# Sparse attention and a routed MLP on one core: batch 0 with a pair's values one pair behind its scores, v of batches 2 and 3 loaded behind the weights, values woven denser with w1 matmuls

## The chip, the cores and the metric

The kernel runs on one core of a Trainium2 chip. The metric is the device time of one execution in microseconds (us). A core has five engines that run their own instruction streams in order: TensorE (PE, matmuls and transposes), VectorE (DVE), ScalarE (ACT), GpSimd (POOL) and SyncE (SP). Here POOL issues all loads from HBM, through one DMA queue, and SP issues the stores and a few copies inside SBUF, through another.

## The reference

There are 4 batches, 8 heads of 64, and 768 positions. Each position attends to its neighbours closer than 16 and to 24 summaries, one per block of 32 positions (the maximum of the block's keys, the mean of its values, each weighted by 32). The 8 heads side by side make x of 768 x 512. The mean of x over the positions picks one of 8 experts per batch, and the output is a two-layer MLP of that expert.

```python
k_sum = k.reshape(B, H, nb, block, D).max(axis=3)
v_sum = v.reshape(B, H, nb, block, D).mean(axis=3)
...
scores_all = np.concatenate([scores_l_m, scores_s], axis=-1)   # window of 16 each way, and 24 summaries
...
a = a / (np.sum(a, axis=-1, keepdims=True) + 1e-09)
x = np.matmul(a, np.concatenate([v, v_sum], axis=2))           # then heads side by side
...
e_idx = np.argmax(x.mean(axis=1) @ w_gate, axis=1)             # one expert a batch
out[b] = gate_w[b] * (np.maximum(x[b] @ w1[e], 0.0) @ w2[e])
```

## The kernel before

The schedule is written out by hand: every step is a Python closure that emits instructions for several engines, and the order in which the closures are called is the order on each engine. `run` calls a list of steps; `weave(main, fill)` calls the steps of `main` and spreads those of `fill` evenly behind them.

Heads are worked on in pairs (4 pairs a batch), positions in two halves of 384 (`u`). The steps of a batch `b` are:

- `T_k(b, pr)`, `T_q(b, pr)`: 16 PE transposes into PSUM (`kps`, `qps`), and a copy out (`kaug`, `qT`; ACT, or for part of the keys of later batches DVE).
- `K_rest`: on DVE the block maxima of the keys (`kmx`, L271) and three copies that complete `kaug` (halos and summaries, L277 to L283).
- `S_tile(b, pr, u)`: scores in PSUM (`sc`: the mask by L350, the products by L362), then the exponential on ACT into `aT` (L372).
- `V_sum`: block sums of the values on PE (`vsps`, L300) and a DVE cast (L309). `V_copy(b, pr)`: a DVE copy of those sums into the rows of `vblk` that the values matmul reads (L315).
- `O_tile(b, pr, u)`: 12 matmuls of `aT` with `vblk` (`ops`, L386), then on DVE the reciprocal (`rv`, L394) and the product (`xs`, L397).
- `X_tile`: three PE transposes of `xs` (`xps`, L413), and an ACT copy into `xT` that also sums over positions (L414).
- `gate(b)`: 8 small matmuls (`lgps`, L427), the expert's index on DVE, and then POOL issues the loads of that expert: `w1` in four pieces (L453), whatever `between` says, and `w2` in two (L457).
- `H_chunk` (16 a batch: 4 matmuls, `hps`, L492, and a relu on ACT, or on DVE for one in four, L501) and `O_chunk` (12 a batch: 4 matmuls, `o_ps`, L515; every second one scales and stores 128 rows).

`vblk` holds values as rows of 64 positions with a halo of 16 rows on either side. For batch 0 the values come pair by pair (L104), and the halo rows are copied inside SBUF by SP (`halo`, L125 and L129) once a pair's values have landed. For later batches POOL loads the values in two halves (L104) and then both halos from HBM (L114, L118): `load_vs`. There are two `vblk` and two `kaug` buffers; `edges` writes their constant rows. PSUM has 2 buffers for `sc` and 4 for all else.

`warm` issues matmuls on a tile of zeros; their results are overwritten. Batch 0 is attention alone; from batch 1 on, the attention of batch `b+1` is woven with the MLP of batch `b`, and the MLP of batch 3 ends the program. After the last `gate` nothing is woven.

Of the kernel before, what the change touches and what calls it, by code (L numbers as in the profile page):

```python
# [22 lines left out]
def kernel(  # L23
# [10 lines left out]
    nc = tc.nc  # L34
# [105 lines left out]
    load_q(0, 0, 2)  # L140
    load_v(0, 0, 2)
# [14 lines left out]
    load_k(0, 2, 4)  # L156
    load_q(0, 2, 4)
    load_v(0, 4, 6)
    load_v(0, 6, 8)
    for pr in range(2, NP):  # L160
        load_k(0, 2 * pr, 2 * pr + 2)
        load_q(0, 2 * pr, 2 * pr + 2)
# [6 lines left out]
    def edges(i):  # L169

        nc.vector.memset(vblks[i][0:QB, :, :, D:DP], 1.0)
        nc.vector.memset(vblks[i][R_SUM:NR, :, :, D:DP], float(BLK))
        nc.vector.memset(vblks[i][QB:R_SUM, :, :, D:DP], 1.0)
        nc.vector.memset(vblks[i][QB:R_SUM, :, 0:1, 0:D], 0.0)
        nc.vector.memset(vblks[i][QB:R_SUM, :, NJ - 1 : NJ, 0:D], 0.0)
        nc.vector.memset(kaugs[i][:, :, 0:1, R_PRE:R_POST], 0.0)
        nc.vector.memset(kaugs[i][:, :, NJ - 1 : NJ, R_POST:R_SUM], 0.0)
        nc.vector.memset(kaugs[i][:, :, :, NR:128], 0.0)

    edges(0)  # L180
# [109 lines left out]
    def V_sum(b, prs):  # L290
        def f():
            vb = vblks[b % NV]
            if b == 0:
                halo(b, 2 * prs[0], 2 * prs[-1] + 2)
            vs_ps = one_pool.tile([128, 2, D], FP32, name="vsps", tag="one")
            if b == 0:
                warm(vs_ps.rearrange("p h c -> p (h c)"), 2, 128)
            for j in range(NJ):
                for pr in prs:
                    nc.tensor.matmul(  # L300
                        vs_ps[BLK * pr : BLK * (pr + 1), :, :],
                        lhsT=bind[:, j, :],
                        rhs=vb[0:QB, 2 * pr : 2 * pr + 2, j, 0:D],
                        start=(j == 0),
                        stop=(j == NJ - 1),
                    )
# [28 lines left out]
    def S_tile(b, pr, u):  # L335
        def f():
# [3 lines left out]
            if b == 0:  # L340
# [34 lines left out]
    def O_tile(b, pr, u):  # L375
        def f():
# [3 lines left out]
            if b == 0:  # L380
                warm(ops.rearrange("p t h c -> p (t h c)"), 1)
# [165 lines left out]
    a0 = [first_warm, T_k(0, 0), *pair_keys(0)]  # L547
    for pr in range(NP):
        more = pr + 1 < NP
        a0 += [S_tile(0, pr, 0), S_tile(0, pr, 1)]  # L550
        a0 += [T_k(0, pr + 1)] if more else []
        a0 += [O_tile(0, pr, 0), O_tile(0, pr, 1)]
        a0 += pair_keys(pr + 1) if more else []
        a0 += [X_tile(0, pr, 0), X_tile(0, pr, 1)]
# [48 lines left out]
    run(s1[:14])  # L603
# [50 lines left out]
```

## Time and profile before

| | |
|---|---|
| median of 2 runs | 195.38 us (194.44 to 196.32) |
| the profiled execution: its time, and its span | 196.97 us, 194.9 us |
| PE busy, share of the span | 165.7 us, 85% |
| DVE, ACT, POOL busy | 92.6 us, 91.8 us, 47.1 us |
| mean granted clock of PE | 0.939 |
| last gate matmul starts, batch 0, 1, 2, 3 | 39.21, 78.15, 119.86, 159.21 us |

Times in the views are microseconds from the start of the span. A row of the timeline gives the start, the length, the engine, the line, the operation, its tiles (out<-in), how many instructions are merged (x12), and in brackets the idle time of that engine before it and what ended the wait. The four gates cut the execution into stages: batch 0 alone, three stages in which attention of one batch is woven with the MLP of the one before, and the rest of the MLPs.

### The profile page before, as it was taken

The page shows a single profiled execution, that of the slowest core. Times are in us where ns is not written, and L with a number is a line of the kernel's source. Part 1 is how long each engine was busy: PE and PEld are TensorE (multiplying, and loading weights), DVE is VectorE, ACT ScalarE, POOL GpSimd, SP SyncE. Part 2 cuts the span into 40 slices and gives each one's busy share as a digit, 9 for nine tenths or more (in the row PEclk, how much of TensorE's full clock was granted, in tenths as well). Part 3 has the DMA queues.
Part 4 walks back from the last instruction along what each step waited for, and adds up shares of the span by engine and source line. Part 5 has one row for each costly group of instructions (what it writes and reads, how often), then busy time and mean ns, then how long its engine had stood idle before and what let it go on. Part 6 is the DMA issues. An engine that isn't in the chain of part 4 may idle for free.

```text
span 194.9 us, 5234 instructions
## 1 busy us (share of the span) xinstructions
PE 165.7 (85%) x2242; PEld 95.9 (49%) x2257; DVE 92.6 (47%) x249; ACT 91.8 (47%) x187; POOL 47.1 (24%) x65
## 2 busy tenths in 40 slices
PE   7497988859987698989959998799969989979991
PEld 2355556547444365455525565455635644545440
DVE  5625475475036463768214853975257533121211
ACT  2132656748764066265831555466634651436120
POOL 7980000049700000497000000990000008000000
PEclk9998599975699799999996999999999999999999
DMA  4999950019999996399999991799998016999142
GB/s 45 149 172 222 215 93 3 0 20 139 158 101 95 203 207 120 57 151 187 194 123 200 206 175 62 111 157 203 177 157 148 3 55 105 168 274 156 54 161 108
DMA packets 57382, 26.00 MB, mean 133 GB/s; under 512 B 39696, under 2 KB 54288, under 8 KB 57360
## 3 DMA queue, kind: packets, MB, share of 16 engines
q0 software_dynamic: 52992, 19.00, 112.4%
q1 hardware_dynamic: 4368, 6.68, 11.4%
q8 instruction: 17, 0.28, 0.6%
q14 instruction: 5, 0.04, 0.1%
HBM read 38.00 MB, written 6.29 MB: 227 GB/s over the span
## 4 chain that ended last, share of the span: by engine, by line
DMA 36%; PE 35%; POOL 8%; issue 8%; DVE 5%; ACT 4%; POOLq 2%; SPq 0%; DVEq 0%; ACTq 0%
DMA vblk<-in_v_dram 27%; PE hps L492 12%; PE o_ps L515 8%; DMA w_sb<-in_moe_w_dram 6%; PE ops L386 5%; DMA vblk<-vblk 3%; POOL w_sb L453 3%; POOL vblk L104 3%; PE xps L413 2%; ACT xT L414 2%; PE vsps L300 2%; PE sc L229 1%; ACT qT L250 1%; ACT o_sb L530 1%; POOLq L439 1%
## 5 line engine op out<-in xcount | busy, mean ns | idle before, releaser
L492 PE MATMUL hps<-xT,w_sb 128*128 128x384 bf16 x256 | 50.7, 344 | 1.5 <-DMA w_sb<-in_moe_w_dram 1.3
L515 PE MATMUL o_ps<-w_sb,hT 128*128 128x512 bf16 x177 | 43.9, 380 | 1.6 <-issue 1.3
L453 POOL DMA_DIRECT2D w_sb<-in_moe_w_dram x16 | 12.0, 760 | 115.4 <-DVE grec L468 55.3
L503 ACT ACTIVATE hT<-hps 128x384 bf16<-128x384 f32 x48 | 23.4, 493 | 34.4 <-PE hps L492 34.1
L372 ACT ACTIVATE aT<-sc 128x768 bf16<-128x768 f32 x32 | 25.7, 811 | 16.1 <-PE sc L362 16.0
L492 PEld LDWEIGHTS <-w_sb 128*128 128x128 bf16 x256 | 23.6, 101 | 18.0 <-issue 3.1
L515 PEld LDWEIGHTS <-hT 128*128 128x128 bf16 x192 | 16.6, 98 | 17.3
L501 DVE TENSOR_SCALAR hT<-hps 128x384 bf16<-128x384 f32 x16 | 8.9, 558 | 26.6 <-PE hps L492 26.6
L250 ACT COPY qT<-qps 128x768 bf16<-128x768 bf16 x16 | 12.8, 797 | 14.2 <-PE qps L241 14.1
L414 ACT ACTIVATE xT<-xps 128x384 bf16<-128x384 bf16 x32 | 15.6, 489 | 7.1 <-PE xps L413 6.9
L525 DVE TENSOR_SCALAR o_sb<-o_ps,gcol 128x512 f32<-128x512 f32 x12 | 9.0, 751 | 20.5 <-PE o_ps L515 20.5
L397 DVE TENSOR_TENSOR xs<-ops,rv 128x384 bf16<-128x384 f32 x32 | 17.8, 558 | 1.1
L394 DVE RECIPROCAL rv<-ops 128x6 f32<-128x6 f32 x32 | 6.2, 193 | 22.4 <-PE ops L386 22.4
L386 PE MATMUL ops<-vblk,aT 120*64 120x65 bf16 x384 | 11.9, 202 | 5.5 <-DMA vblk<-in_v_dram 4.1
L530 ACT ACTIVATE o_sb<-o_ps,gcol 128x512 f32<-128x512 f32 x12 | 8.3, 688 | 17.2 <-PE o_ps L515 11.3
L362 PE MATMUL sc<-qT,kaug 64*128 64x64 bf16 x384 | 12.4, 204 | 4.2 <-DVE kaug L283 4.2
L271 DVE TENSOR_REDUCE kmx<-kps 128x24 bf16<-128x768 bf16 x16 | 15.1, 945 | 0.1
L386 PEld LDWEIGHTS <-aT 120*64 120x64 bf16 x384 | 8.7, 113 | 12.3 <-issue 8.3
L362 PEld LDWEIGHTS <-kaug 64*128 64x128 bf16 x384 | 9.2, 105 | 6.9 <-DVE kaug L283 5.0
L300 PE MATMUL vsps<-vblk,bind 64*32 64x128 bf16 x192 | 7.7, 231 | 5.7 <-DMA vblk<-in_v_dram 5.7
L413 PE MATMUL xps<-identb,xs 128*128 128x128 bf16 x96 | 10.3, 225 | 2.3 <-ACT qT L250 1.8
L104 POOL DMA_DIRECT2D vblk<-in_v_dram x10 | 12.1, 1228 | 0.0
(74 smaller groups left out, 181.2 us busy)
## 6 DMA issues: line engine op xcount, KB each, us to landing
w_sb<-in_moe_w_dram POOLq DMA_DIRECT2D x12, 512.0 KB, 16.5
out_dram<-o_sb SPq DMA_DIRECT2D x24, 256.0 KB, 5.0
k_nat<-in_k_dram POOLq DMA_DIRECT2D x3, 768.0 KB, 22.7
q_nat<-in_q_dram POOLq DMA_DIRECT2D x3, 768.0 KB, 25.0
vblk<-in_v_dram POOLq DMA_DIRECT2D x6, 384.0 KB, 13.5
vblk<-in_v_dram POOLq DMA_DIRECT2D x6, 190.0 KB, 17.5
w_sb<-in_moe_w_dram POOLq DMA_DIRECT2D x8, 128.0 KB, 4.1
w_sb<-in_moe_w_dram POOLq DMA_DIRECT2D x4, 256.0 KB, 6.2
```

The lines of the kernel that those rows point to most:

```text
L104: nc.gpsimd.dma_start(vb[0:QB, h0:h1, :, 0:D].rearrange("p h j d -> p (h j) d"), v[b, h0:h1].rearrange("h (j p) d -> p (h j) d", p=QB),)
L250: nc.scalar.copy(out_, in_)
L271: nc.vector.tensor_reduce(out=kmx, in_=kpss.pop((b, pr)).rearrange("q r (n p) -> q n r p", n=NB), axis=AX.XY, op=ALU.max,)
L362: nc.tensor.matmul(sc[:, hh, w * QB : (w + 1) * QB], lhsT=ka[rs, pr, j, :], rhs=qT[rs, j * QB : (j + 1) * QB], start=False, stop=w == NW - ...
L372: nc.scalar.activation(aT, sc[:, :, 0:HB], ACT.Exp, scale=SCALE)
L386: nc.tensor.matmul(ops[w * QB : (w + 1) * QB, t, hh, :], lhsT=aT[0:NR, hh, c0 : c0 + QB], rhs=vb[0:NR, 2 * pr + hh, u * NW + 2 * t + w, 0 ...
L397: nc.vector.tensor_tensor(out=xs, in0=ops[:, :, :, 0:D], in1=rv.unsqueeze(3).to_broadcast([128, NW // 2, 2, D]), op=ALU.mult,)
L414: nc.scalar.activation(xT[b][:, pr, u * HB : (u + 1) * HB], xps, ACT.Copy, accum_out=red[b][:, pr, u : u + 1],)
L453: nc.gpsimd.dma_start(w1_sb[:, :, fs], w1_src[:, :, fs])
L492: nc.tensor.matmul(hps[:, 0:HB], lhsT=w1_sb[:, dt, ft * 128 : (ft + 1) * 128], rhs=xT[b][:, dt, u * HB : (u + 1) * HB], start=(dt == 0), s ...
L503: nc.scalar.activation(dst, hps[:, 0:HB], ACT.Relu)
L515: nc.tensor.matmul(o_ps, lhsT=hTs[b][:, ft, st * 128 : (st + 1) * 128], rhs=w2_sb[:, ft, :], start=(ft == 0), stop=(ft == NFT - 1),)
```

## The change

Batch 0 is written as a pipeline over pairs: in step `i` come keys and queries of pair `i`, the transposes of the result of pair `i-2`, the scores of pair `i`, the values of pair `i-1`, and the block sums of pair `i`. Half of its `warm` matmuls in the scores go, those in `V_sum` go, those of the values are put together. Keys and queries of pair 1 are loaded ahead of the values of pairs 0 and 1. `edges(1)` moves from DVE to POOL. In later batches `V_copy` of a pair stands directly ahead of that pair's first `O_tile`, no longer all four behind `V_sum`. In the stage of batch 1 the w1 matmuls start to be woven earlier. In the stages of batches 2 and 3, `load_vs` stands behind both halves of `w2`, and more `H_chunk`s stand ahead of `V_sum`.

```diff
     load_q(0, 0, 2)
+    load_k(0, 2, 4)
+    load_q(0, 2, 4)
     load_v(0, 0, 2)
     load_v(0, 2, 4)
...
-            if b == 0:
-                warm(vs_ps.rearrange("p h c -> p (h c)"), 2, 128)
...
-            if b == 0:
+            if b == 0 and u == 0:
                 warm(sc[:, 0], 2)
...
-            if b == 0:
-                warm(ops.rearrange("p t h c -> p (t h c)"), 1)
+            if b == 0 and u == 0:
+                warm(ops.rearrange("p t h c -> p (t h c)"), 2)
...
-    a0 = [first_warm, T_k(0, 0), *pair_keys(0)]
-    for pr in range(NP):
-        more = pr + 1 < NP
-        a0 += [S_tile(0, pr, 0), S_tile(0, pr, 1)]
-        a0 += [T_k(0, pr + 1)] if more else []
-        a0 += [O_tile(0, pr, 0), O_tile(0, pr, 1)]
-        a0 += pair_keys(pr + 1) if more else []
-        a0 += [X_tile(0, pr, 0), X_tile(0, pr, 1)]
+    a0 = [first_warm]
+    for i in range(NP + 2):
+        if i < NP:
+            a0 += [T_k(0, i), T_q(0, i), K_rest(0, i)]
+        if i >= 2:
+            a0 += [X_tile(0, i - 2, 0), X_tile(0, i - 2, 1)]
+        if i < NP:
+            a0 += [S_tile(0, i, 0), S_tile(0, i, 1)]
+        if 1 <= i <= NP:
+            a0 += [V_copy(0, i - 1), O_tile(0, i - 1, 0), O_tile(0, i - 1, 1)]
+        if i < NP:
+            a0 += [V_sum(0, [i])]
...
-        st = [V_sum(b, list(range(NP)))] + [V_copy(b, pr) for pr in range(NP)]
+        st = [V_sum(b, list(range(NP)))]
         units = [(pr, u) for pr in range(NP) for u in range(2)]
         for i in range(len(units) + 2):
             if i < len(units):
+                if units[i][1] == 0:
+                    st.append(V_copy(b, units[i][0]))
                 st.append(O_tile(b, *units[i]))
...
-    run(a0[:20])
-    edges(1)
-    run(a0[20:])
+    edges(1, nc.gpsimd)
+    run(a0)
...
-    run(s1[:14])
+    run(s1[:8])
-    weave(hs[0][0:6], s1[14:])
-    run(hs[0][6:8])
-    weave(hs[0][8:16] + os_[0][0:2], values(1))
-    gate(1, lambda: load_vs(2))
+    weave(hs[0][0:9], s1[8:])
+    run(hs[0][9:10])
+    weave(hs[0][10:16] + os_[0][0:2], values(1))
+    gate(1, lambda: None)
+    load_vs(2)
...
-            weave(os_[b - 1][2:12], scores(b + 1))
-            run(hs[b][0:5])
-            weave(hs[b][5:16] + os_[b][0:2], values(b + 1))
-            gate(b + 1, (lambda: load_vs(3)) if b == 1 else (lambda: None))
+            run(os_[b - 1][2:5])
+            weave(os_[b - 1][5:12] + hs[b][0:4], scores(b + 1))
+            run(hs[b][4:8])
+            weave(hs[b][8:16] + os_[b][0:2], values(b + 1))
+            gate(b + 1)
+            if b == 1:
+                load_vs(3)
```

Lines behind the edits move by one: L386 is L385 after the change, L453 and L457 are L452 and L456, L492 is L491.

On DVE, in batch 0, from the key maxima of the first pair on, before the change (`kmx`, `kaug` are keys, `vs_sb`, `vblk` block sums of the values, `rv`, `xs` the result of a half):

```order
L271 TENSOR_REDUCE kmx<-kps 128x24
L277 COPY kaug_89<-kaug_89 128x11x16
L280 COPY kaug_89<-kaug_89 128x11x16
L283 COPY kaug_89<-kmx 128x12x24
L309 CAST vs_sb<-vsps 32x128
L315 COPY vblk_87<-vs_sb 24x24x64
L394 RECIPROCAL rv<-ops 128x6
L397 TENSOR_TENSOR xs<-ops,rv 128x384
```

and at the same place after it:

```order
L272 TENSOR_REDUCE kmx<-kps 128x24
L278 COPY kaug_89<-kaug_89 128x11x16
L281 COPY kaug_89<-kaug_89 128x11x16
L284 COPY kaug_89<-kmx 128x12x24
L308 CAST vs_sb<-vsps 32x128
L272 TENSOR_REDUCE kmx<-kps 128x24
L278 COPY kaug_89<-kaug_89 128x11x16
L281 COPY kaug_89<-kaug_89 128x11x16
L284 COPY kaug_89<-kmx 128x12x24
L314 COPY vblk_87<-vs_sb 24x24x64
L393 RECIPROCAL rv<-ops 128x6
L396 TENSOR_TENSOR xs<-ops,rv 128x384
```

The keys of the second pair now stand ahead of the first pair's block-sum copy and its results.

On POOL, behind the gate of batch 1, from the last piece of w1 on, before (`vblk` loads are the values of batch 2, `k_nat`, `q_nat` the keys and queries of batch 3):

```order
L453 DMA w_sb<-in_moe_w_dram 128x4x512
L104 DMA vblk_87<-in_v_dram 64x48x64 x2
L114 DMA vblk_87<-in_v_dram 16x95x64
L118 DMA vblk_87<-in_v_dram 16x95x64
L457 ISA
L457 DMA w_sb<-in_moe_w_dram 128x4x512
L457 ISA
L457 DMA w_sb<-in_moe_w_dram 128x4x512
L91 DMA k_nat<-in_k_dram 96x8x512
```

and after:

```order
L452 DMA w_sb<-in_moe_w_dram 128x4x512
L456 ISA
L456 DMA w_sb<-in_moe_w_dram 128x4x512
L456 ISA
L456 DMA w_sb<-in_moe_w_dram 128x4x512
L104 DMA vblk_87<-in_v_dram 64x48x64 x2
L114 DMA vblk_87<-in_v_dram 16x95x64
L118 DMA vblk_87<-in_v_dram 16x95x64
L91 DMA k_nat<-in_k_dram 96x8x512
```

The two halves of w2 have moved ahead of the four loads of values. The same holds behind the gate of batch 2.

On DVE, in the values of batch 2, from the cast of the block sums on, before (`hT` is the relu of a w1 chunk):

```order
L309 CAST vs_sb<-vsps 128x128
L315 COPY vblk_87<-vs_sb 24x24x64 x2
L501 TENSOR_SCALAR hT<-hps 128x384
L315 COPY vblk_87<-vs_sb 24x24x64 x2
L394 RECIPROCAL rv<-ops 128x6
L397 TENSOR_TENSOR xs<-ops,rv 128x384
```

and after:

```order
L308 CAST vs_sb<-vsps 128x128
L314 COPY vblk_87<-vs_sb 24x24x64
L393 RECIPROCAL rv<-ops 128x6
L396 TENSOR_TENSOR xs<-ops,rv 128x384
L393 RECIPROCAL rv<-ops 128x6
L396 TENSOR_TENSOR xs<-ops,rv 128x384
L314 COPY vblk_87<-vs_sb 24x24x64
L393 RECIPROCAL rv<-ops 128x6
L396 TENSOR_TENSOR xs<-ops,rv 128x384
L500 TENSOR_SCALAR hT<-hps 128x384
```

Three of the four block-sum copies now stand between the results of the pairs. Further on, the last of them stands behind the relu of the last w1 chunk.

More of the change, by code (lines that the diff above doesn't have):

```diff
@@ L155 @@
     )
-    load_k(0, 2, 4)
-    load_q(0, 2, 4)
+    load_k(0, 4, 6)
+    load_q(0, 4, 6)
     load_v(0, 4, 6)
     load_v(0, 6, 8)
-    for pr in range(2, NP):
-        load_k(0, 2 * pr, 2 * pr + 2)
-        load_q(0, 2 * pr, 2 * pr + 2)
+    load_k(0, 6, 8)
+    load_q(0, 6, 8)
     load_k(1)
@@ L167, with edges @@
     nc.sync.dma_start(wg_sb, moe_w_gate.rearrange("(g p) e -> p g e", p=128))
[L169 to L180, printed above, removed]
+    def edges(i, eng):
+        eng.memset(vblks[i][0:QB, :, :, D:DP], 1.0)
+        eng.memset(vblks[i][R_SUM:NR, :, :, D:DP], float(BLK))
+        eng.memset(vblks[i][QB:R_SUM, :, :, D:DP], 1.0)
+        eng.memset(vblks[i][QB:R_SUM, :, 0:1, 0:D], 0.0)
+        eng.memset(vblks[i][QB:R_SUM, :, NJ - 1 : NJ, 0:D], 0.0)
+        eng.memset(kaugs[i][:, :, 0:1, R_PRE:R_POST], 0.0)
+        eng.memset(kaugs[i][:, :, NJ - 1 : NJ, R_POST:R_SUM], 0.0)
+        eng.memset(kaugs[i][:, :, :, NR:128], 0.0)
+    edges(0, nc.vector)
     ones_row = const.tile([1, 128], FP32, name="ones_row")
@@ L537, in moe @@
         ]
-    def pair_keys(pr):
-        return [K_rest(0, pr), V_sum(0, [pr]), V_copy(0, pr), T_q(0, pr)]
     def first_warm():
```

## The prediction

> **What bounds the kernel now.** I read the chain that ended last on the page first, then the chain in order of time, then PE's timeline at the places where the chain leaves the compute engines. The page's shares by line begin with the values:
>
> ```profile
> DMA vblk<-in_v_dram 27%; PE hps L492 12%; PE o_ps L515 8%; DMA w_sb<-in_moe_w_dram 6%; PE ops L386 5%; DMA vblk<-vblk 3%; POOL w_sb L453 3%; POOL vblk L104 3%; PE xps L413 2%; ACT xT L414 2%; PE vsps L300 2%; PE sc L229 1%; ACT qT L250 1%; ACT o_sb L530 1%; POOLq L439 1%
> ```
>
> The chain in order of time shows where these lie (start, length, what):
>
> ```profile
> 9.88 6.28 DMA vblk<-vblk
> ...
> 48.17 16.88 DMA vblk<-in_v_dram
> ...
> 85.09 17.30 DMA vblk<-in_v_dram
> ...
> 128.61 17.83 DMA vblk<-in_v_dram
> ```
>
> So each woven stage is held by its own load of values: the chain goes from the gate over POOL to the values and only then back to PE. PE's timeline tells how long PE really stood there:
>
> ```profile
> 65.19 0.43 PE L386 MATMUL ops<-vblk,aT 120*64 120x65 bf16 x12 [3.03 <-DMA vblk<-in_v_dram]
> ...
> 78.15 0.20 PE L427 MATMUL lgps<-wg_sb,red 128*1 128x8 f32 x2 [0.28 <-ACT xT L414]
> ...
> 95.80 4.07 PE L492 MATMUL hps<-xT,w_sb 128*128 128x384 bf16 x24
> 99.81 0.23 PE L300 MATMUL vsps<-vblk,bind 64*32 64x128 bf16 x2
> 102.43 1.06 PE L300 MATMUL vsps<-vblk,bind 64*32 64x128 bf16 x46 [2.40 <-DMA vblk<-in_v_dram]
> ...
> 106.94 0.38 PE L386 MATMUL ops<-vblk,aT 120*64 120x65 bf16 x12
> ...
> 119.86 0.20 PE L427 MATMUL lgps<-wg_sb,red 128*1 128x8 f32 x2 [0.28 <-ACT xT L414]
> ...
> 141.56 0.23 PE L300 MATMUL vsps<-vblk,bind 64*32 64x128 bf16 x2
> 142.60 0.84 PE L300 MATMUL vsps<-vblk,bind 64*32 64x128 bf16 x46 [0.81 <-DMA vblk<-in_v_dram]
> ...
> 146.58 0.38 PE L386 MATMUL ops<-vblk,aT 120*64 120x65 bf16 x12 [1.08 <-DMA vblk<-in_v_dram]
> ...
> 159.21 0.20 PE L427 MATMUL lgps<-wg_sb,red 128*1 128x8 f32 x2 [0.28 <-ACT xT L414]
> ```
>
> PE waits 3.03 us in the stage of batch 1, 2.40 in that of batch 2, 0.81 + 1.08 in that of batch 3. In the last two PE arrives at the values almost when they land: there is no slack for a later landing. And from the first values matmul to the gate (106.94 to 119.86, 146.58 to 159.21) PE hardly waits, so a delay there passes through to the end.
>
> **The part that costs: w2 ahead of the values.** POOL's queue works in the order of issue. In the stage of batch 2, the two loads of w2 now stand behind the last halo load (the answers for L457 and L118 in that stretch):
>
> ```profile
> L457 POOL DMA_DIRECT2D w_sb<-in_moe_w_dram x2: 807/824/841, 88.2 to 89.0; - x2
> DMA to landing us min/median/max: 20.5/21.4/22.3
> ...
> L118 POOL DMA_DIRECT2D vblk<-in_v_dram x1: 943/943/943, 87.4 to 87.4; - x1
> DMA to landing us min/median/max: 19.5/19.5/19.5
> ```
>
> The halos land at 87.4 + 19.5 = 106.9, which is when the first values matmul runs, and the second half of w2 at 89.0 + 22.3 = 111.3. Putting w2 ahead pushes values and halos back by the difference, 4.4 us. Nothing gets shorter in exchange: w2 is first read by an `O_chunk` behind the last w1 chunk, where it has long landed. Issue by POOL (0.8 us each) is no part of it, since the queue lags 19 us behind.
>
> Against that stands PE work moved ahead of `V_sum`: 9 chunks of w1 instead of 6. A chunk is 4.07 / 6 = 0.68 us, so `V_sum` is reached at 99.8 + 2.0 = 101.9 instead of 99.8, while its second half of values lands at 102.4 + 4.4 = 106.8: a wait of 4.9 instead of 2.4. Behind `V_sum` (1.1) and one chunk PE stands again, until the halos at 111.3. So the first values matmul moves by 4.4 us, from 106.9 to 111.3, and in the stage of batch 3 from 146.6 to 151.0. From there one chunk fewer is left than now (6, not 7): -0.7 us.
>
> Then the values themselves. The copies of block sums now stand on DVE between the pairs:
>
> ```profile
> L397 DVE TENSOR_TENSOR xs<-ops,rv 128x384 bf16<-128x384 f32 x32 | 17.8, 558 | 1.1
> L394 DVE RECIPROCAL rv<-ops 128x6 f32<-128x6 f32 x32 | 6.2, 193 | 22.4 <-PE ops L386 22.4
> ...
> L315 DVE COPY vblk<-vs_sb x16: 552/553/557, 10.8 to 146.1; 24x1536 bf16<-24x1536 bf16 x16
> ...
> L501 DVE TENSOR_SCALAR hT<-hps 128x384 bf16<-128x384 f32 x16 | 8.9, 558 | 26.6 <-PE hps L492 26.6
> ```
>
> Pair 1's first values matmul waits for its copy, which stands behind both results of pair 0: 2 x (0.19 + 0.56) + 0.55 = 2.1 us from the end of pair 0's first half. PE has 0.3 (second half) + 0.7 (one chunk) to do meanwhile, so it stands 1.1 us. Pair 2's copy is covered by two chunks. Pair 3's stands behind the relu of the last chunk: 0.56 + 0.55 = 1.1 us plus a hop, with nothing in between: 1.2 us. Queued behind these waits on PE are the rest of the values and so the gate. Together +2.3 us; zero if PE finds the copies done (bound below), 2.3 is what the order on DVE gives, and I take it.
>
> Per stage 4.4 - 0.7 + 2.3 = **+6.0 us, twice: +12.0**. Without the copies it would be 3.7 a stage.
>
> **The clock behind the longer waits** (stretches of one 3.41 us window; PE busy, then the other engines, the granted clock, DMA share and GB/s):
>
> ```profile
> 21.00:24.41 3.41, 3.41 (x52) 1.89 (x50) 1.09 (x6) 1.89 (x4) 0.00 (x0) 0.50 1.24 207
> 24.41:41.48 17.07, 14.26 (x316) 9.55 (x312) 9.91 (x31) 11.03 (x25) 0.00 (x0) 1.00 0.16 28
> ...
> 44.90:48.31 3.41, 3.41 (x76) 2.77 (x78) 2.61 (x5) 2.66 (x5) 3.41 (x4) 0.50 1.19 143
> ...
> 99.51:102.92 3.41, 1.01 (x41) 0.58 (x42) 0.00 (x0) 0.73 (x2) 0.00 (x0) 1.00 3.85 88
> 102.92:106.33 3.41, 3.41 (x36) 1.66 (x24) 1.53 (x4) 0.49 (x1) 0.00 (x0) 0.50 1.28 211
> 142.60:147.00 4.40, 3.32 (x71) 2.17 (x71) 3.07 (x7) 0.98 (x2) 0.00 (x0) 1.00 1.62 182
> ```
>
> After a window in which PE was busy for 1.01 us the next runs at 0.50; the stage of batch 3 keeps 1.00 now. With waits of 4.9 and 3.5 us both will drop. Half a clock over one window is up to 1.7 us of PE work; part falls into the second wait and the copy stalls. I count 0, and 0 to 1.4 a stage for the range.
>
> **Batch 0.** The rows that carry it:
>
> ```profile
> 6.91 0.64 POOL L91 DMA_DIRECT2D q_nat<-in_q_dram  x1
> ...
> 13.76 0.51 PE L362 MATMUL sc<-qT,kaug 64*128 64x64 bf16 x12
> 16.30 0.38 PE L386 MATMUL ops<-vblk,aT 120*64 120x65 bf16 x12 [1.30 <-DMA vblk<-vblk]
> ...
> 36.93 0.38 PE L386 MATMUL ops<-vblk,aT 120*64 120x65 bf16 x12
> 39.21 0.20 PE L427 MATMUL lgps<-wg_sb,red 128*1 128x8 f32 x2 [0.24 <-ACT xT L414]
> ...
> 28.05:34.05 6.00, 5.32 (x115) 3.62 (x115) 3.55 (x11) 4.11 (x9) 0.00 (x0) 1.00 0.01 3
> ...
> L413 PE MATMUL xps<-identb,xs 128*128 128x128 bf16 x7 | 0.9, 219 | 1.3 <-ACT qT L250 1.3
> L372 ACT ACTIVATE aT<-sc 128x768 bf16<-128x768 f32 x2 | 1.6, 812 | 0.3 <-PE sc L362 0.2
> ```
>
> A pair takes 6.0 us at full clock now, of which PE is busy 5.3; the rest is a wait for ACT's copy of the queries. The pipeline has scores, values of the pair before and block sums to put there, and drops about 0.7 us of zero matmuls: 4.6 us a pair for PE. ACT has the same: two copies (1.6), two exponentials (1.6), two results (1.4), so 4.6 it is. Worked through: pair 0's scores end at 13.5 (now 14.3; a zero pair and the block sums are gone from in front, two more loads of 0.64 stand ahead of the masks on POOL), its block sums at 14.8; pair 1's step without results of an earlier pair is 4.1 us at full clock, some 7.5 at half, to 22.3; the halo copies (6.3 us, now the end of a 1.30 wait) are covered by pair 1's scores; pairs 2 and 3 at 4.6 each, to 31.5; pair 3's cast, copy and values 2.1; and from the end of the last values to the gate what it takes now, 39.4 - 37.3 = 2.1. The gate comes at 35.7 instead of 39.4: **-3.7 us**. This needs the clock back at about 22, as a gap-free window gave it back at 24.41. If it comes a window sooner, 5.2 are won; if pair 2 runs at half clock too, nothing.
>
> A window full of matmuls is not enough: 44.90 to 48.31 has PE busy throughout, with scores and transposes, and the clock stays at 0.50. [...]
>
> `edges(1)` on POOL costs nothing: POOL then idles for most of 27.87 us ahead of L453. If its eight fills (0.27 us at most on DVE) held DVE up, 2 us at the worst, in pair 1.
>
> ```profile
> 41.55 3.03 POOL L453 DMA_DIRECT2D w_sb<-in_moe_w_dram  x4 [27.87 <-DVE grec L468]
> ...
> L174 DVE MEMSET vblk<- x2: 272/272/272, 2.1 to 21.2; 32x256 uint32 x2
> ```
>
> **The stage of batch 1** keeps the order of its loads, so the halos land where they do, relative to the gate. The w1 chunks woven earlier only fill time ahead of the 3.03 us wait. Behind it one chunk fewer (-0.7, or -1.4 at half clock) stands against copy stalls of 0.3 to 1.6: 0, with -1.4 to +1.
>
> **Sum:** -3.7 + 0 + 12.0 = +8.3 us. Against the profiled execution, 196.97 us (194.9 of span and 2.1 around it), 205.3; it lies 1.6 above the median of the runs shown, 195.38, from which it is 203.7. I predict **203.7**.
>
> **The rivals.**
> - *w2 does not push the values back.* The values move only 88 GB/s in the window before 102.92, other windows 207 to 211, so there is room if both ran side by side. Against it: w2 and the halos landed in the order of issue. Then the stages change by -0.7 to +1.6 each, and with batch 0 the time is 195.4 - 3.7 - 1.4 = 190 to 195. It decides for "not slower" from a push of less than about 1.5 us. Chance 0.15.
> - *Batch 0 stays at half clock.* Each of pairs 2 and 3 then takes about 8.4 instead of 4.6 us; one of them eats the gain (207.5), both give 211. Speaks for it: 16 zero matmuls fewer in batch 0, and row 44.90. Against: scores, values and block sums now follow each other without a gap. Chance 0.15.
> - *The copies find cover* (waits for the halos and the half clock swallow the DVE stalls) and batch 0 gains 5: 195.4 - 5 + 2 x 3.7 = 198, within 2%. Chance 0.15.
>
> **How the numbers follow.** The forecast has 0.55. Lowest sum without the first rival: -5.2 - 1.4 + 2 x 3.7 = +0.8; highest: 0 + 1 + 2 x 7.4 = +15.8. I leave out the first rival and the top of the second: 197 to 209.5. Two per cent (3.9 us) is about what a measurement here can tell from no change. Faster takes 0.11 from the first rival; same its rest and the third's most, 0.18; slower 0.71.
>
> **What would show it.** Right: the gate of batch 0 near 35.7; in the stages of batches 2 and 3 the halo loads landing last of values and w2, some 31 us behind the stage's first w1 load, `V_sum` waiting 3 to 5 us, 0.50 behind it, PE idle ahead of the first half of pairs 1 and 3 with DVE's L314 as the one that ends it, and stages 6 us longer. Wrong: halos that land within 27 us of the first w1 load, or a gate of batch 0 behind 38.

## The result, and the profile after

The changed kernel takes **217.62 us** (median of 2 runs, 216.26 and 218.98) against 195.38: ratio 1.114, 95% interval 1.076 to 1.152. On the chip of runs 5 to 8 below the pair was run again: 215.52 us (214.79 to 222.18, 5 runs) against 199.97 (192.75 to 206.24, 19 runs), ratio 1.097 (1.069 to 1.124). The ratios leave out executions more than 1.5% slower than the fastest of the same kernel; the medians hold all of them. The forecast was 203.7, its range ended at 209.5: the sign was right, the size was not.

The profiled execution took 218.98 us, of which 216.9 are span, with a mean granted clock of 0.841. From gate to gate (us):

| | batch 0 | batch 1 | batch 2 | batch 3 | rest |
|---|---|---|---|---|---|
| before | 39.4 | 38.9 | 41.7 | 39.4 | 35.5 |
| after | 39.2 | 38.6 | 51.7 | 51.2 | 36.2 |
| forecast of the difference | -3.7 | 0 | +6.0 | +6.0 | 0 |
| measured | -0.2 | -0.4 | +10.0 | +11.9 | +0.7 |

All of the loss lies in the stages of batches 2 and 3. The page of the profile gives the shares by line of the chain that ended last: the values stand at 32% now (27% before), and the copy of block sums is a new name in it (`DVE vblk L314`):

```profile
DMA vblk<-in_v_dram 32%; PE hps L491 8%; PE o_ps L514 8%; DMA w_sb<-in_moe_w_dram 5%; PE ops L385 5%; DMA vblk<-vblk 4%; DVE xs L396 3%; POOL vblk L104 3%; PE xps L412 2%; ACT xT L413 2%; DVE vblk L314 2%; POOL w_sb L452 2%; DMA out_dram<-o_sb 1%; POOL vblk L114 1%; PE vsps L299 1%
```

PE's timeline of the changed kernel, the stage of batch 2 from gate to gate and three rows of the next (start, busy time, line, tiles, in brackets the idle time ahead and who ended it):

```profile
77.61 0.20 PE L426 MATMUL lgps<-wg_sb,red 128*1 128x8 f32 x2 [0.28 <-ACT xT L413]
...
102.61 0.23 PE L299 MATMUL vsps<-vblk,bind 64*32 64x128 bf16 x2 [1.90 <-DMA vblk<-in_v_dram]
106.93 1.46 PE L299 MATMUL vsps<-vblk,bind 64*32 64x128 bf16 x46 [4.10 <-DMA vblk<-in_v_dram]
...
111.65 0.87 PE L385 MATMUL ops<-vblk,aT 120*64 120x65 bf16 x24 [1.86 <-DMA vblk<-in_v_dram]
...
114.34 0.54 PE L385 MATMUL ops<-vblk,aT 120*64 120x65 bf16 x12 [0.42 <-DVE vblk L314]
...
124.03 0.38 PE L385 MATMUL ops<-vblk,aT 120*64 120x65 bf16 x12 [1.22 <-DVE vblk L314]
...
129.32 0.19 PE L426 MATMUL lgps<-wg_sb,red 128*1 128x8 f32 x2 [0.28 <-ACT xT L413]
...
158.82 1.46 PE L299 MATMUL vsps<-vblk,bind 64*32 64x128 bf16 x46 [3.86 <-DMA vblk<-in_v_dram]
...
162.86 0.87 PE L385 MATMUL ops<-vblk,aT 120*64 120x65 bf16 x24 [1.19 <-DMA vblk<-in_v_dram]
...
175.23 0.38 PE L385 MATMUL ops<-vblk,aT 120*64 120x65 bf16 x12 [1.22 <-DVE vblk L314]
```

What was forecast for this stage is there: the wait ahead of the second half of `V_sum`, the first values matmul at 111.65 (forecast 111.3), the two waits for copies. The length of the half clock is what was not. The same stretch in windows of 3.41 us, the length for which the clock was at 0.50 in this stage of the kernel before (102.92 to 106.33; here it is 17.07, from 103.68 to 120.75, five times that). A row gives length, busy time of PE, PEld, DVE, ACT and POOL, granted clock, DMA share and GB/s:

```profile
103.68:107.09 3.41, 0.16 (x8) 0.16 (x11) 0.00 (x0) 0.00 (x0) 0.00 (x0) 0.50 5.24 79
107.09:110.51 3.42, 2.70 (x50) 1.47 (x42) 0.84 (x2) 0.49 (x1) 0.00 (x0) 0.50 2.52 123
110.51:113.92 3.41, 2.27 (x28) 1.17 (x28) 1.60 (x5) 0.00 (x0) 0.00 (x0) 0.50 1.25 205
113.92:117.33 3.41, 2.99 (x33) 1.81 (x34) 1.87 (x5) 1.07 (x3) 0.00 (x0) 0.50 0.90 149
117.33:120.75 3.42, 3.42 (x26) 1.88 (x25) 1.28 (x3) 1.45 (x4) 0.00 (x0) 0.50 0.05 8
```

Five windows at 0.50, where before had one. The clock comes back at 120.75, behind the first window that PE fills (3.42 us); the three ahead of it have 2.70, 2.27 and 2.99 us of PE work, and holes: 0.72 and 1.14 us are the wait for the halos, 0.42 is the wait for the copy of pair 1. A group of 12 values matmuls that took 0.38 us takes 0.54 meanwhile. The stage of batch 3 repeats this from 154.9 to 171.9.

### The profile page after: what moved, and what is told of

Its sections match the earlier page's. It is cut to its first block, busy times and chain, and to the rows that moved or that the text cites. A ratio compares the mean times of both kernels' runs of the same rounds, so it can differ in the third digit from the quotient of the medians.

```text
span 216.9 us, 5197 instructions
## 1 busy us (share of the span) xinstructions
PE 173.5 (80%) x2230; PEld 99.2 (46%) x2241; DVE 90.6 (42%) x241; ACT 91.1 (42%) x187; POOL 49.2 (23%) x73
## 4 chain that ended last, share of the span: by engine, by line
DMA 42%; PE 29%; DVE 8%; POOL 8%; issue 6%; ACT 4%; POOLq 1%; SPq 0%
DMA vblk<-in_v_dram 32%; PE hps L491 8%; PE o_ps L514 8%; DMA w_sb<-in_moe_w_dram 5%; PE ops L385 5%; DMA vblk<-vblk 4%; DVE xs L396 3%; POOL vblk L104 3%; PE xps L412 2%; ACT xT L413 2%; DVE vblk L314 2%; POOL w_sb L452 2%; DMA out_dram<-o_sb 1%; POOL vblk L114 1%; PE vsps L299 1%
## 5 line engine op out<-in xcount | busy, mean ns | idle before, releaser
L491 PE MATMUL hps<-xT,w_sb 128*128 128x384 bf16 x256 | 56.9, 368 | 2.0 <-DMA w_sb<-in_moe_w_dram 2.0
L502 ACT ACTIVATE hT<-hps 128x384 bf16<-128x384 f32 x48 | 23.3, 494 | 46.2 <-PE hps L491 45.8
L452 POOL DMA_DIRECT2D w_sb<-in_moe_w_dram x16 | 12.0, 764 | 131.6 <-PE o_ps L514 80.1
L491 PEld LDWEIGHTS <-w_sb 128*128 128x128 bf16 x256 | 24.3, 106 | 19.1 <-issue 5.0
L371 ACT ACTIVATE aT<-sc 128x768 bf16<-128x768 f32 x32 | 25.3, 812 | 12.5 <-PE sc L361 12.5
L385 PE MATMUL ops<-vblk,aT 120*64 120x65 bf16 x384 | 13.3, 222 | 10.7 <-DMA vblk<-in_v_dram 5.0
L385 PEld LDWEIGHTS <-aT 120*64 120x64 bf16 x384 | 10.4, 132 | 20.9 <-issue 7.8
L299 PE MATMUL vsps<-vblk,bind 64*32 64x128 bf16 x192 | 8.9, 272 | 12.2 <-DMA vblk<-in_v_dram 12.2
L396 DVE TENSOR_TENSOR xs<-ops,rv 128x384 bf16<-128x384 f32 x32 | 17.8, 557 | 1.1
L272 DVE TENSOR_REDUCE kmx<-kps 128x24 bf16<-128x768 bf16 x16 | 15.2, 947 | 3.4 <-ACT kaug L251 3.3
L251 ACT COPY qT<-qps 128x768 bf16<-128x768 bf16 x16 | 12.8, 799 | 7.5 <-PE qps L242 7.5
L299 PEld LDWEIGHTS <-bind 64*32 64x32 bf16 x192 | 7.0, 120 | 13.8 <-issue 8.6
L253 DVE COPY kaug<-kps 128x768 bf16<-128x768 bf16 x10 | 9.5, 952 | 8.8 <-PE kps L242 8.7
## 6 DMA issues: line engine op xcount, KB each, us to landing
vblk<-in_v_dram POOLq DMA_DIRECT2D x6, 190.0 KB, 22.6
```

Of the source, the lines that this page charges most:

```text
L251: nc.scalar.copy(out_, in_)
L272: nc.vector.tensor_reduce(out=kmx, in_=kpss.pop((b, pr)).rearrange("q r (n p) -> q n r p", n=NB), axis=AX.XY, op=ALU.max,)
L299: nc.tensor.matmul(vs_ps[BLK * pr : BLK * (pr + 1), :, :], lhsT=bind[:, j, :], rhs=vb[0:QB, 2 * pr : 2 * pr + 2, j, 0:D], start=(j == 0), ...
L371: nc.scalar.activation(aT, sc[:, :, 0:HB], ACT.Exp, scale=SCALE)
L385: nc.tensor.matmul(ops[w * QB : (w + 1) * QB, t, hh, :], lhsT=aT[0:NR, hh, c0 : c0 + QB], rhs=vb[0:NR, 2 * pr + hh, u * NW + 2 * t + w, 0 ...
L396: nc.vector.tensor_tensor(out=xs, in0=ops[:, :, :, 0:D], in1=rv.unsqueeze(3).to_broadcast([128, NW // 2, 2, D]), op=ALU.mult,)
```

## The experiments

Two theories stood against each other. **L**: the late values make PE wait, and that long wait alone drops the clock for five windows. **C**: the copies between the pairs stall PE and so keep the clock at half. The twelve runs (the kernel before beside runs 1 to 4: 200.56; beside 5 to 8: 199.97; beside 9 to 12: 199.61):

| run | median us (range) | stages of batches 0 to 3 and rest |
|---|---|---|
| 1 a_vbetween | 206.93 (205.63-207.02) | 38.2 40.2 45.4 45.2 36.2 |
| 2 b_vlast | 210.69 (209.56-216.37) | 40.7 36.0 48.2 48.2 36.1 |
| 3 a_copies | 209.19 (205.30-210.76) | 38.6 35.2 47.3 45.0 37.2 |
| 4 a_hold | 216.15 (211.46-217.26) | 38.5 39.0 48.6 52.6 36.5 |
| 5 b_copies | 212.81 (209.16-218.23) | 40.7 42.4 46.2 44.4 36.3 |
| 6 a_both | 196.77 (192.57-198.07) | 39.5 37.2 42.5 40.6 36.3 |
| 7 a_same | 215.52 (214.79-222.18) | 38.8 41.4 52.2 49.0 38.9 |
| 8 a_bothw | 196.45 (194.01-200.09) | 39.7 37.0 40.0 40.2 35.1 |
| 9 a_bothw1 | 196.38 (192.60-198.05) | 38.1 34.7 41.4 40.7 35.8 |
| 10 b_early | 189.25 (188.63-194.22) | 40.6 35.6 37.6 38.1 35.3 |
| 11 a_early | 193.66 (192.12-194.67) | 37.7 35.9 39.6 39.6 37.3 |
| 12 a_bothe | 191.25 (188.86-192.81) | 37.8 36.8 38.0 38.0 36.2 |

The kernel before itself ranges over 13 us, so the arguments below go by stages of the profiled executions; 1 or 2 us in one stage of one run prove nothing. The profiled execution took 217.24 us in run 4, 198.07 in run 6 and 222.18 in run 7; in the other runs it lies within 4 us of the median.

**1. The loads put back** (in the changed kernel, values between w1 and w2 again).

```diff
-    gate(1, lambda: None)
-    load_vs(2)
+    gate(1, lambda: load_vs(2))
...
-            gate(b + 1)
-            if b == 1:
-                load_vs(3)
+            gate(b + 1, (lambda: load_vs(3)) if b == 1 else (lambda: None))
```

> The changed kernel with the values of batches 2 and 3 loaded between w1 and w2 again; all else as changed. Theory L (the later values make the wait, and the wait drops the clock for five windows): the first values matmul of batch 2 comes about 26.5 us behind the stage's first w1 load instead of 32, no half-clock stretch of 17 us is left, the stages of batches 2 and 3 shrink from 51.7 and 50.9 to about 42 each, total 198 to 200 us. Theory C (the block-sum copies between the pairs hold PE up, and these gaps keep the clock at half): only the direct 4.5 us a stage are won back, the long half-clock stretches stay, total 208 to 210 us.

206.93 us. The stages of batches 2 and 3 lose 6.3 and 6.0 us against the changed kernel and stay some 4 to 6 above before. The halos are back in time, and the stall ahead of the first values matmul is one:

```profile
101.27 0.86 PE L299 MATMUL vsps<-vblk,bind 64*32 64x128 bf16 x48
106.03 0.87 PE L385 MATMUL ops<-vblk,aT 120*64 120x65 bf16 x24 [3.15 <-DMA vblk<-in_v_dram]
...
118.35 0.38 PE L385 MATMUL ops<-vblk,aT 120*64 120x65 bf16 x12 [1.22 <-DVE vblk L314]
```

But from the first values matmul to the gate it still takes 17.8 us (17.1 in the stage of batch 3; before 13.1 and 12.8), at 0.50 for three windows (104.76 to 115.00). The total lies between what L and C had named. Not all is L.

**2. The late loads alone** (in the kernel before).

```diff
-    gate(1, lambda: load_vs(2))
+    gate(1, lambda: None)
+    load_vs(2)
...
-            gate(b + 1, (lambda: load_vs(3)) if b == 1 else (lambda: None))
+            gate(b + 1)
+            if b == 1:
+                load_vs(3)
```

> The kernel before with one edit: the values of batches 2 and 3 loaded behind w2. Theory L: stages of batches 2 and 3 grow by 6 us or more each, a half-clock stretch opens in both, total 207 to 212 us. Theory C: the wait costs its 4.4 us a stage but the gap-free w1 chunks behind it bring the clock back after one window, total 203 to 205 us. If the order of loads did not matter: 195 us.

210.69 us, 10.1 above before: the two stages are 6.5 and 8.8 us longer. PE waits longer than in the changed kernel (4.22 and 4.27 us against 1.90 and 4.10), since six w1 chunks stand ahead of `V_sum` here and nine there:

```profile
102.28 0.29 PE L300 MATMUL vsps<-vblk,bind 64*32 64x128 bf16 x2 [4.22 <-DMA vblk<-in_v_dram]
106.84 1.46 PE L300 MATMUL vsps<-vblk,bind 64*32 64x128 bf16 x46 [4.27 <-DMA vblk<-in_v_dram]
111.83 0.38 PE L386 MATMUL ops<-vblk,aT 120*64 120x65 bf16 x12
```

By the numbers named ahead this is L: stages longer by 6 us or more, 207 to 212 us in all, and half clock behind the waits (46 matmuls of `V_sum` take 1.46 us, where run 1 has 48 in 0.86). The rows place the time elsewhere. From the first values matmul to the gate it takes 13.0 us (before 13.1): the half clock was over ahead of that matmul, whose group of 12 takes 0.38 us (0.54 at half clock in the changed kernel) and ran 0.5 us behind the landing of the halos at 111.3 (0.9 in the stage of batch 3). So here the late landing cost its delay and little clock, with dense work behind the wait: three w1 chunks stand between `V_sum` and the first values, in the changed kernel one. L's second half falls.

**3. The copies put back** (in the changed kernel, directly behind `V_sum`).

```diff
-        st = [V_sum(b, list(range(NP)))]
+        st = [V_sum(b, list(range(NP)))] + [V_copy(b, pr) for pr in range(NP)]
...
-                if units[i][1] == 0:
-                    st.append(V_copy(b, units[i][0]))
```

> The changed kernel with all four block-sum copies directly behind V_sum again; values still behind w2. Theory C: PE no longer waits for L314 between the pairs (1.6 us a stage), the clock comes back two to four windows sooner, total 206 to 210 us. Theory L: the stalls of 1.6 us a stage go and the half clock stays four or five windows, total 213 to 215 us.

209.19 us, within the 206 to 210 that C names. First values matmul to gate: 11.0, 12.5 and 12.1 us in the three stages, where the changed kernel has 14.1, 17.9 and 17.9. PE waits 2.69 and 4.74 us ahead of the two parts of `V_sum` and not at all for the halos; the third window is nearly filled (3.32 us), and the clock is back after it (24 values matmuls take 0.57 us at 110.10, 0.87 at half clock in the changed kernel):

```profile
99.40:102.80 3.40, 0.26 (x2) 0.07 (x3) 0.00 (x0) 0.00 (x0) 0.00 (x0) 0.50 5.24 74
102.80:106.20 3.40, 1.81 (x48) 1.44 (x48) 0.29 (x1) 0.00 (x0) 0.00 (x0) 0.50 3.26 106
106.20:109.63 3.43, 3.32 (x22) 1.50 (x21) 2.60 (x6) 0.98 (x2) 0.00 (x0) 0.50 1.33 201
```

The edit moves one thing more. `weave` deals fill steps by their count, so with the four copies ahead of them the first values stand behind two w1 chunks after `V_sum`, in the changed kernel behind one. The second chunk is part of what fills the third window and of why no wait for the halos is left. No run moves the copies alone: what is called the copies' price in runs 1, 3, 5 and 6 is that of the copies and of this shift.

**4. The clock held** (in the changed kernel, zero matmuls of 512 columns: 24 ahead of `V_sum`, 12 ahead of the first values matmul, in the stages of batches 2 and 3).

```diff
+    def hold(n):
+        warm(sc_pool.tile([128, 2, 512], FP32, name="sc", tag="sc")[:, 0], n, 512)
...
+            if b >= 2 and pr == 0 and u == 0:
+                hold(12)
...
             run(hs[b][4:8])
+            hold(24)
```

> The changed kernel with matmuls on zeros added in the stages of batches 2 and 3: 24 of 512 columns ahead of V_sum (5.2 us at full clock) and 12 ahead of the first values matmul (2.6 us), so that PE does not idle while it waits for the values. The order of loads and copies is unchanged. If the half clock is a cost of its own, it stays at 1.00 through these stages and each is 3 to 4.5 us shorter, total 209 to 212 us; what is left above 195 is then the late landing and the copies. If the clock does not matter, the total stays at 217 or grows.

216.15 us. In the stage of batch 2 it did what it should: a granted clock of 1.00 throughout, the first values matmul where it was (33.8 us behind the gate), and waits for the copies of 1.20 and 1.22 us (0.42 and 1.22 in the changed kernel):

```profile
103.70:120.75 17.05, 13.30 (x190) 7.34 (x190) 7.93 (x19) 5.05 (x14) 0.00 (x0) 1.00 1.85 112
```
```profile
111.22 0.57 PE L390 MATMUL ops<-vblk,aT 120*64 120x65 bf16 x24
113.75 0.38 PE L390 MATMUL ops<-vblk,aT 120*64 120x65 bf16 x12 [1.20 <-DVE vblk L314]
...
120.62 0.38 PE L390 MATMUL ops<-vblk,aT 120*64 120x65 bf16 x12 [1.22 <-DVE vblk L314]
```

From there to the gate 14.9 us instead of 17.9: **the half clock costs 3.0 us** in this stage, the copies' two waits 2.4. In the stage of batch 3 it failed by its own doing. A wait of 2.24 us was left behind the zero matmuls, and the clock was at 0.50 from 156.25 to 163.08; the second dozen ran in it and took 4.66 us (2.75 in the stage of batch 2), 3.5 us past the landing of the halos at 160.3. That is why the total gained nothing. But the clock was back when the first values came (24 values matmuls in 0.57 us at 163.83), and from there to the gate this stage takes 14.9 us too, again 3.0 less than in the changed kernel.

```profile
156.60 1.46 PE L299 MATMUL vsps<-vblk,bind 64*32 64x128 bf16 x46 [2.24 <-DMA vblk<-in_v_dram]
...
159.25 4.66 PE L230 MATMUL sc<-zb 128*128 128x512 bf16 x12
```

**5. The copies alone** (in the kernel before; the diff of run 3 the other way round).

> The kernel before with only the block-sum copies moved between the pairs; loads, batch 0 and weaving as before. If the copies cost their stalls alone (1.1 to 1.2 us ahead of pairs 1 and 3), the stretch from the first values matmul to the gate grows from 13.1 and 12.8 us to 15.1 to 15.5 in the stages of batches 2 and 3, and the time by 4 to 6 us against the kernel before. If they also hold the clock at half behind the wait for the values, the stretch is 17 us or more, the half clock lasts 10 us or more there instead of 3.4, and the time grows by 8 to 12 us. If the copies cost something only together with values that land late, the stretches stay within 0.7 us of before.

212.81 us, 12.8 above before. From the first values matmul to the gate it takes 17.4, 18.0 and 18.0 us in the three stages, 4.3 to 5.1 more than before; in the stage of batch 2 half clock lasts two windows (0.50 from 107.97 to 114.80). What adds to the waits here is the weaving: with the copies no longer at the front of the list the values start after one w1 chunk instead of three. Nine chunks are then left behind the halos, before had seven, while PE waits for the halos:

```profile
107.79 1.32 PE L492 MATMUL hps<-xT,w_sb 128*128 128x384 bf16 x4
111.30 0.54 PE L386 MATMUL ops<-vblk,aT 120*64 120x65 bf16 x12 [2.19 <-DMA vblk<-in_v_dram]
...
119.56 0.38 PE L386 MATMUL ops<-vblk,aT 120*64 120x65 bf16 x12 [1.22 <-DVE vblk L315]
```

**6. Both put back**, so that the new batch 0 and the earlier w1 chunks are what is left of the change (the diffs of runs 1 and 3 together).

> The changed kernel with both suspects put back: values loaded between w1 and w2, and the four copies directly behind V_sum. What is left of the change is the new order of batch 0 and the w1 chunks woven earlier. If the two suspects explain all of the loss, the stages of batches 2 and 3 are back at 39 to 42 us, the halos land 26 to 28.5 us behind the gate, first values matmul to gate is 11 to 12.5 us (one chunk fewer, no stall), and the time is that of the kernel before, -3 to +2 us. If the earlier w1 chunks themselves lengthen PE's wait and so drop the clock, half clock lasts 10 us behind V_sum, and the time stays 4 to 8 us above.

196.77 us against 199.97, ratio 0.983 (0.969 to 0.997): the same or a little faster, which this interval does not decide. Stages of 42.5 and 40.6 us; in that of batch 2 half clock is over soon (12 values matmuls take 0.54 us at 109.61 and 0.38 at 111.29). No stage is more than 1.7 us from the kernel before. So the loss goes with the loads and the copies together; a cost of the new batch 0 or of the denser weaving does not show.

**7. The changed kernel again.**

> The changed kernel again, unaltered, beside the others on one chip. Its stages of batches 2 and 3 are to be 50 to 52 us with five windows of half clock each if that length of half clock is what the change makes by itself; if it is chance from run to run, stages of 47 to 49 us with 7 to 10 us of half clock appear here. Time 8 to 14 per cent above the kernel before.

215.52 us; stages of 52.2 and 49.0 us, and a mean granted clock of 0.834 in the profiled execution (0.841 in that of the result). The long stages belong to the change; that of batch 3 is 2.2 us shorter here. With runs 1, 3 and 6 the loss splits roughly, by medians over the kernel before: copies +6.4 (run 1), late loads +8.6 (run 3), both +15.6.

**8. and 9. Zero matmuls in batch 0** (on top of run 6; run 8 has two ahead of every unit of scores and values, run 9 only in the first pair and the scores of the second).

Run 8, in the units of scores and of values alike:

```diff
-            if b == 0 and u == 0:
+            if b == 0:
```

> As the run with both suspects put back, and in batch 0 two zero matmuls of 384 columns ahead of every unit of scores and of values (16 more in all, 2.6 us of PE at full clock, 5.3 at half). If it is the half clock until 28.6 us that eats the gain of the new batch 0, the clock returns at 22 to 25 us and the gate of batch 0 comes at 36 to 37.5 us. If PE's own work bounds batch 0, the gate moves back to 40.5 to 43. If the waits on DVE (keys with sums, 0.9 us in each of pairs 1 and 3) and on the halo copies bound it, the zero matmuls lie in them and the gate stays at 38 to 39.5.

Run 9, first in the units of scores, then in those of values:

```diff
-            if b == 0 and u == 0:
+            if b == 0 and pr <= 1:
...
-            if b == 0 and u == 0:
+            if b == 0 and pr == 0:
```

> Both suspects put back (values between w1 and w2, copies behind V_sum), and zero matmuls ahead of every unit only in the first pair and the scores of the second pair of batch 0, none added later. If the half clock until 28.6 us is what eats the gain of batch 0, the clock returns at 21 to 24 us as it does with zero matmuls everywhere, and then pairs 2 and 3 take 5.2 us each (4.3 of PE work and 0.96 of waiting for the keys with sums): gate of batch 0 at 37 to 38. If the rest of batch 0 is bound by DVE and the end of the last pair, the gate stays at 38.5 to 39.5 although the clock is back.

Run 8: the clock is back before 22 us (12 values matmuls take 0.54 us at 20.79 and 0.38 at 21.77), but the gate stays at 39.7: with the added zero matmuls a pair takes 6.3 us even at full clock. Run 9: back at 22.4 (0.50 from 8.80 to 22.40, 1.00 to 32.70), and the gate at 38.1. Its block sums, one `V_sum` per pair, and the gate:

```profile
22.55 0.84 PE L299 MATMUL vsps<-vblk,bind 64*32 64x128 bf16 x12
...
27.32 0.84 PE L299 MATMUL vsps<-vblk,bind 64*32 64x128 bf16 x12
...
32.19 1.04 PE L299 MATMUL vsps<-vblk,bind 64*32 64x128 bf16 x12
...
37.91 0.20 PE L426 MATMUL lgps<-wg_sb,red 128*1 128x8 f32 x2 [0.24 <-ACT xT L413]
```

At full clock a pair takes 4.8 us (forecast 4.6), of which PE waits 1.3 for the keys with their sums; pairs 2 and 3 have no zero matmuls here. With the added zero matmuls pair 1's step ends at 23.4 instead of 22.6, and behind 32.7 the clock is at 0.50 again (32.70 to 46.30), so that 1.1 us is what remains. Neither kernel's time can be told from that of run 6.

**10. The values a stage earlier** (in the kernel before: v of batch b+1 is loaded behind the keys and queries of batch b+1, one stage ahead of its use).

```diff
     edges(1)
+    load_vs(1)
...
-    gate(0, lambda: load_vs(1))
+    gate(0, lambda: None)
     load_k(2)
     load_q(2)
+    load_vs(2)
...
-    gate(1, lambda: load_vs(2))
+    gate(1, lambda: None)
     load_k(3)
     load_q(3)
+    load_vs(3)
...
-            gate(b + 1, (lambda: load_vs(3)) if b == 1 else (lambda: None))
+            gate(b + 1, lambda: None)
```

> The kernel before with the values of batches 1, 2 and 3 loaded one stage earlier: behind the queries and keys of batch 1 while batch 0 runs, and behind those of batches 2 and 3 in the stages of batches 1 and 2. If PE's wait for the landing of the values (and the half clock behind it) is what the stages of before lose, PE finds the values landed: no wait ahead of V_sum or the first values matmul, no half clock there, stages of 34 to 37 us instead of 39 to 42, and 8 to 15 us less than the kernel before. If the landing is only one of several bounds (w1 becomes the late load, or the transfers of the values push w1 back), the stages stay at 38 to 41 and the time within 4 us of before.

**189.25 us** against 199.61, ratio 0.949 (0.939 to 0.960): faster than both kernels. PE never waits for values in the stages of batches 2 and 3, and the granted clock is 1.00 throughout them (PE busy 35.9 of 37.6 and of 38.1 us):

```profile
76.20:113.81 37.61, 35.88 (x555) 20.51 (x556) 22.63 (x55) 21.18 (x45) 10.55 (x12) 1.00 1.92 170
113.81:151.86 38.05, 35.92 (x555) 20.59 (x556) 22.35 (x55) 21.23 (x45) 4.50 (x6) 1.00 0.62 103
```

**11. and 12. The same loads in the changed kernel**, with its copies between the pairs (run 11), and with the copies behind `V_sum` and the zero matmuls of run 9 (run 12).

> The changed kernel, copies between the pairs and its batch 0 included, with the values loaded one stage earlier as in the run above. If the copies cost their order on DVE alone (1.2 us ahead of pairs 1 and 3) once no long wait drops the clock, the stages are 1 to 3 us longer than those of the same loads with the copies behind V_sum, at full clock throughout, and the time is 8 to 20 us below that of the changed kernel, near or under before. If the copies by themselves keep the clock at half, half clock of 7 us or more appears in the stages of batches 2 and 3 without any wait for a load, and they stay at 42 us or more.

> The changed kernel with the values one stage earlier, the copies directly behind V_sum, and two zero matmuls ahead of every unit of the first pair and of every unit of scores of the second in batch 0. It is the candidate for a faster version: stages of batches 1, 2 and 3 of 34 to 36.5 us each and a gate of batch 0 at 37 to 39, together 180 to 188 us. Against the changed kernel with only the loads moved it shows the price of the copies: 2 to 3 us a stage if they cost stalls alone, 5 if they cost clock too.

193.66 us (0.974, 0.964 to 0.984) and 191.25 (0.963, 0.953 to 0.972); run 12 misses the 180 to 188 that it was to reach. Run 11 keeps the two waits for copies and has a granted clock of 1.00 in both stages (73.64 to 113.21, 113.21 to 152.77):

```profile
100.84 0.38 PE L385 MATMUL ops<-vblk,aT 120*64 120x65 bf16 x12 [1.20 <-DVE vblk L314]
...
107.72 0.38 PE L385 MATMUL ops<-vblk,aT 120*64 120x65 bf16 x12 [1.22 <-DVE vblk L314]
```

Its stages are 1.6 us longer than those of run 12 (39.6 against 38.0), with the same 36.0 us of PE work in each. So here the copies between the pairs do not drop the clock: with their shift in the weaving they cost 1.6 us. In runs 1 and 5, where the clock was at 0.50 behind a long wait, first values matmul to gate took 4.3 to 5.1 us more than before. Run 10 and run 12 overlap in their times; which of them is faster stays open.

## Why the prediction was wrong

Its sum was +8.3 us on the profiled execution; it came to +22.0. The difference of 13.7 lies in three of its terms, and a rest of 0.3.

- **The clock behind the waits, counted 0 (0 to 1.4 a stage): about 3 a stage. This step failed.** I priced one window of 3.41 us, because one is what the kernel before showed, and let the second wait and the copy stalls swallow it. The rows show five windows at 0.50 in either stage, and 1.00 again only behind one with 3.42 us of PE work (run 3: behind 3.32). The holes in the windows ahead of it were first the rest of the wait for the halos (1.86 us over two windows, behind a single w1 chunk; 2.70 and 2.27 us of PE work), then the copy of pair 1 (0.42; 2.99). The sum has them as delay and as stalls, and not as holes with more half clock behind them. The first values matmul to the gate grew by 4.8 and 5.0 us, forecast 1.6 each; run 4 gives 3.0 to the clock in either stage. The later landing was not needed for it: with the loads in the old order (run 1) the same stretch still takes 17.8 and 17.1 us. I added terms that are not independent: the wait for the halos and the stall ahead of pair 1 lie inside the half clock. How much of the 3.0 is due to the copies themselves, and how much to the w1 chunk that their shift takes from the front, stays open.
- **The push by w2, 4.4 us: 5.3 and 6.8.** Direction and place were read rightly: the halos land last, 33.8 us behind the gate. The size came from the landings of halos and w2 in the old order, the tail of w2 behind the halos. Ahead of them it takes longer; the loads of w1 (L452), w2 (L456) and the last halo (L118) in the changed kernel:

```profile
L452 POOL DMA_DIRECT2D w_sb<-in_moe_w_dram x4: 747/754/762, 79.7 to 82.1; - x4
...
DMA to landing us min/median/max: 3.4/6.4/10.4
```
```profile
L456 POOL DMA_DIRECT2D w_sb<-in_moe_w_dram x2: 770/774/777, 82.8 to 83.6; - x2
...
DMA to landing us min/median/max: 13.0/14.1/15.3
```
```profile
L118 POOL DMA_DIRECT2D vblk<-in_v_dram x1: 961/961/961, 87.9 to 87.9; - x1
...
DMA to landing us min/median/max: 23.7/23.7/23.7
```

  w1 is in at 82.1 + 10.4 = 92.5, w2 at 98.9: 6.4 us, not 4.4; the halos at 111.6. In the stage of batch 3 w2 takes 7.0. The push is not this alone: w1 was in 1.3 and 1.0 us later behind the gate than before, and the halos came 12.7 and 11.4 us behind w2, before 15.2 and 12.5 behind w1. My guess is that part of w2 had gone beside the halos in the old order, so that its tail was a lower bound that I took for the value; no run shows the two side by side. The forecast of the first values matmul hit by luck (111.3 against 111.65): the gate ahead of it came 0.5 us earlier.
- **Batch 0, -3.7: -0.2.** Pair 1's step ended at 22.6 (forecast 22.3). The condition that I named, the clock back at about 22, was not met: it came at 28.59, so pair 2 took 6.7 us instead of 4.6. Pair 3, at full clock, took 5.3 with a wait of 0.96 for the keys, and the end 4.7 instead of 4.2. Together 0.3 + 2.1 + 0.7 + 0.5 = 3.5 (differences of rounded times). The second rival, which I gave 0.15, came half true. The length of a pair was near, 4.8 us where run 9 had the clock, but partly by luck: 1.3 of it is a wait for the keys that the sum leaves out, and run 9 has the four zero matmuls of a pair less.

```profile
21.76:25.17 3.41, 3.41 (x49) 2.71 (x47) 1.81 (x5) 1.68 (x3) 0.00 (x0) 0.50 1.24 219
25.17:28.59 3.42, 3.42 (x61) 2.09 (x61) 1.38 (x7) 2.29 (x6) 0.00 (x0) 0.50 0.86 144
28.59:38.83 10.24, 7.58 (x174) 5.41 (x172) 6.90 (x19) 6.15 (x16) 0.00 (x0) 1.00 0.02 3
```
```profile
32.12 0.35 PE L361 MATMUL sc<-qT,kaug 64*128 64x64 bf16 x12 [0.96 <-DVE kaug L284]
```

What held: the copies' waits (forecast 1.1 and 1.2; at full clock 1.20 and 1.22), `V_sum`'s wait (4.9; 4.1 behind another 1.9), the stage of batch 1 (0; -0.4, though of two parts that cancel: first values 1.3 us sooner behind the gate, 1.0 more from there on), and that nothing gets shorter by w2's earlier landing. That the fills on POOL cost nothing is not shown by itself. The first rival (w2 does not push) and the third (copies find cover, at 198) are refuted by these rows.

## What to carry to other kernels

A wait that ends at half clock is priced with the work behind it: in the stages of batches 2 and 3 of the changed kernel it lasted 17.07 us, until PE was busy for a whole 3.41 us, and it cost 3.0 us a stage beside the waits. So look for the stalls that a change puts into the work behind the wait, and ask of each how much half clock may follow it. In a queue whose loads land in the order of issue, as POOL's did here (w1 at 92.5, w2 at 98.9, the halos at 111.6), price a load that is moved ahead by its own whole transfer (6.4 and 7.0 us here, for pushes of 5.3 and 6.8) rather than by how far it ended behind the others (4.4). A step that is moved in a list which is dealt out by count moves the steps behind it too. And where the longest wait is for a load whose buffer has been free for a stage, issue it a stage earlier before anything around it is reordered: that was worth 5%.

## What the runs showed of the hardware

- In the traces of the two kernels the granted clock was 0.50 for 3.41 us (before, 102.92 to 106.33), 6.82 (before, 17.59 to 24.41), 10.24 (before, 41.48 to 51.72) and 17.07 (changed, 103.68 to 120.75).
- In the stages of batches 2 and 3 of these traces, 0.50 came behind 99.51 to 102.92 of the kernel before, with 1.01 us of PE work, and behind 100.27 to 103.68 and 151.47 to 154.88 of the changed one, with 0.67 and 1.11. It ended behind 102.92 to 106.33 of the kernel before (3.41) and 117.33 to 120.75 and 168.53 to 171.95 of the changed one (3.42 each). The window with the 0.42 us wait for a copy (2.99) was followed by another at 0.50. PE's busy time alone does not tell what follows: 38.07 to 41.48 of the kernel before has 2.38 us and was followed by 0.50, 120.75 to 124.16 of the changed one has 2.19 and was followed by 1.00.
- Nor was a filled window always followed by full clock: 21.76 to 25.17, above, and 44.90 to 48.31 of the kernel before are full and were followed by 0.50, 25.17 to 28.59 is full and was followed by 1.00. Transposes take 2.3 and 2.0 us of the first two. But 11.52 to 14.93 of the changed kernel, with 0.8 us of transposes in 3.24 of PE work, was followed by 0.50 too, and 66.13 to 69.55, with 1.0 in 3.34, by 1.00; what sets them apart no run shows.
- One program's time ranges over 192.75 to 206.24 us in 19 executions on one chip. The stage of batch 1 of run 2, which is the kernel before's, took 36.0 us instead of 38.9.
